# Loading w_out as four adjacent rows to a partition, with stage 1 taking w_in columns at a step of four

## The chip, the cores and the metric

One core of one Trainium2 chip. The time is the device time of one launch in microseconds; each kernel is run several times and the median is quoted with the range. Ratios are the mean time of one kernel's fast runs over the mean time of the other's fast runs of the same rounds, so they are not quite the ratios of the medians quoted beside them; the interval is 95%. A run more than 1.5% above the fastest of its kernel counts as slow and is left out of the ratios. TensorE is called PE in the views, its weight loads PEld, GpSimd POOL, SyncE SP; st, h, o and acc are the names of the tiles that matmuls write.

## The reference

Sliding-window attention (window 64) over q, k, v of 8 batches x 8 heads x 576 positions x 64, then a two-layer block on the 4608 x 512 result:

```python
def _moe_ref(x, w_in, w_out):            # x 4608 x 512, w_in 512 x 2048, w_out 2048 x 512
    h = x @ w_in
    relu6 = np.clip(h + 3.0, 0.0, 6.0)
    g = h * relu6 / 6.0
    return (g @ w_out).astype(np.float32)
```

The change concerns only the two weight matrices. The order of the 2048 hidden columns is free, as long as stage 1 (x @ w_in) and stage 2 (g @ w_out) use the same one.

## The kernel before

Both weights lie in SBUF as bf16, each in one tile, brought by four loads of 1 MB (fp32 in HBM, cast in the DMA) from GpSimd's queue. A w_in load brings a block of 512 columns for all four row groups g; the block's four pieces of a partition therefore lie 2048 elements apart.

```python
win16 = consts.tile([P, NG, FF], BF16, name="win16")       # P = 128, NG = 4, FF = 2048
wout16 = consts.tile([P, NFC, DM], BF16, name="wout16")    # NFC = 16, DM = 512

def load_w_in(f0, f1, g0, g1):
    return nc.gpsimd.dma_start(
        out=win16[:, g0:g1, f0:f1],
        in_=moe_w_in[g0 * P : g1 * P, f0:f1].rearrange("(g p) f -> p g f", p=P))

def load_w_out(c0, c1):
    return nc.gpsimd.dma_start(
        out=wout16[:, c0:c1, :],
        in_=moe_w_out[c0 * P : c1 * P, :].rearrange("(c p) j -> p c j", p=P))
# ... the order on GpSimd's queue (casts between them cut) ...
w_in = [load_w_in(0, 512, 0, NG)]
w_in.append(load_w_in(512, 1024, 0, NG))
w_in.append(load_w_in(1024, 1536, 0, NG))
ld = LoadsForPE(1, nc.gpsimd)
ld.main(0, 0, 4)          # q of the second batch, 512 KB
ld.main(1, 0, 4)          # k, 512 KB
w_in.append(load_w_in(1536, 2048, 0, NG))
ld.rest()
w_out = [load_w_out(0, 4)]
# ... stage 1, for a block T of 512 tokens and a group fc of 128 hidden columns ...
for g in gs:
    nc.tensor.matmul(
        hT, lhsT=win16[:, g, fc * P : (fc + 1) * P],
        rhs=xT[:, g, t0 : t0 + TB], start=(g == 0), stop=(g == NG - 1))
```

The program does not write its waits. A tracker in the framework puts semaphore waits where it sees an instruction touch a stretch of a tile that earlier instructions wrote. That is the author's reading: the compiled lists below show the waits, not how they are found. The order of instructions is fixed by the program.

The softmax here doesn't subtract the row's maximum and nothing guards it: scores larger than these inputs give would overflow.

Of the kernel before, what the change touches and what calls it, by code (L numbers as in the profile page):

```python
# [24 lines left out]
def kernel(  # L25
# [10 lines left out]
    P = nc.NUM_PARTITIONS  # L36
# [191 lines left out]
    win16 = consts.tile([P, NG, FF], BF16, name="win16")  # L228
    wout16 = consts.tile([P, NFC, DM], BF16, name="wout16")

    def load_w_in(f0, f1, g0, g1):
        return nc.gpsimd.dma_start(
            out=win16[:, g0:g1, f0:f1],
            in_=moe_w_in[g0 * P : g1 * P, f0:f1].rearrange("(g p) f -> p g f", p=P),
        )

    def load_w_out(c0, c1):
        return nc.gpsimd.dma_start(
            out=wout16[:, c0:c1, :],
            in_=moe_w_out[c0 * P : c1 * P, :].rearrange("(c p) j -> p c j", p=P),  # L240
        )


# [272 lines left out]
    def s1_bank(fc, T):  # L516
        if T == 0:
            if fc in (6, 7, 14, 15):
                return (ps_o, ps_acc)[fc % 2].tile([P, 512], F32, name=("o", "acc")[fc % 2])[:]
            if fc in (8, 9, 12, 13):  # L520
                return ps_st.tile([P, 2, 512], F32, name=f"st{fc % 2}")[:, 0, :]
            return h_bank()[:]
        if T == 1:
            return turn()
        if T == 2:
            if fc in (8, 9):
                return ps_st.tile([P, 2, 512], F32, name=f"st{fc % 2}")[:, 0, :]
            if fc in (6, 7, 12, 13):
                return (ps_o, ps_acc)[fc % 2].tile([P, 512], F32, name=("o", "acc")[fc % 2])[:]
            return h_bank()[:]  # L530
        if T > 1 and fc < 2:
            return ps_st.tile([P, 2, 512], F32, name=f"st{fc}")[:, 0, :]
        if fc % 4 > 1:
            return h_bank()[:]
        return (ps_o, ps_acc)[fc % 4].tile([P, 512], F32, name=("o", "acc")[fc % 4])[:]
# [3 lines left out]
    def turn(tr=False):  # L539
        i = turns[0] % 6  # L540
        turns[0] += 1
        shape, dt = ([P, 1024], BF16) if tr else ([P, 512], F32)
        if i < 2:
            return ps_h.tile(shape, dt, name=h_name())[:]
        if i < 4:
            return (ps_o, ps_acc)[i - 2].tile(shape, dt, name=("o", "acc")[i - 2])[:]
        return ps_st.tile([P, 2, shape[1]], dt, name=f"st{i - 4}")[:, 0, :]
# [12 lines left out]
    def s1(T, first=()):  # L560
        t0 = T * TB
        gT = gpool.tile([P, NFC, TB], BF16, name="gT")
        gTs[T] = gT

        def mms(fc, hT, gs):
            for g in gs:
                nc.tensor.matmul(  # L567
                    hT, lhsT=win16[:, g, fc * P : (fc + 1) * P],
                    rhs=xT[:, g, t0 : t0 + TB], start=(g == 0), stop=(g == NG - 1),
                )  # L570

        def gate(out, hT, shape):
            t1 = (t1pool, t2pool)[len(shape) - 2].tile(shape, BF16, name=f"t{len(shape) - 1}")
            nc.scalar.activation(out=t1[:], in_=hT, func=RELU, bias=half[:], scale=1.0 / 6.0)  # L574
            nc.vector.scalar_tensor_tensor(  # L575
                out=out, in0=t1[:], scalar=1.0, in1=hT, op0=MIN, op1=MULT,
            )

        if T == 1:
            hTs = [turn() for fc in range(4)]  # L580
            for gs in first:
                for fc in range(4):
                    mms(fc, hTs[fc], gs)
                yield
            for fc in range(4):
                mms(fc, hTs[fc], (NG - 1,))
                gate(gT[:, fc, :], hTs[fc], [P, TB])
                yield
        elif first:
            sts = [ps_st.tile([P, 2, 512], F32, name=f"st{u}") for u in range(2)]  # L590
            for gs in first:
                for fc in range(4):
                    mms(fc, sts[fc // 2][:, fc % 2, :], gs)
                yield
            for u in range(2):
                for fc in (2 * u, 2 * u + 1):
                    mms(fc, sts[u][:, fc % 2, :], (NG - 1,))
                gate(gT[:, 2 * u : 2 * u + 2, :], sts[u][:], [P, 2, TB])
                yield
                yield  # L600
        for fc in range(4 if first else 0, NFC):
            hT = s1_bank(fc, T)
            mms(fc, hT, range(NG))
            gate(gT[:, fc, :], hT, [P, TB])
            yield
# [17 lines left out]
    def s2(T, order):  # L623

        gT, accs = gTs[T], {}
        for ts, f0, f1 in order:
            if T == NTB - 1 and ts == 3:
                yield from last(gT, ts) if f0 == 0 else ()
                continue
            if f0 == 0:  # L630
                accs[ts] = h_bank()[:] if T == 0 and ts < 2 else next(oa)
            for fc in range(f0, f1):
                nc.tensor.matmul(  # L633
                    accs[ts], lhsT=gT[:, fc, ts * P : (ts + 1) * P], rhs=wout16[:, fc, :],
                    start=(fc == 0), stop=(fc == NFC - 1),
                )
            if f1 == NFC:
                osb = osbp.tile([P, DM], F32, name="osb")
                acopy(out=osb[:], in_=accs[ts])  # L639
                u0 = T * TB + ts * P  # L640
                if T:
                    nc.sync.dma_start(out=out[u0 : u0 + P, :], in_=osb[:])
                else:
                    held.append((u0, osb))
            yield
# [62 lines left out]
    for g in range(NG):  # L708
        cast_pairs(bt, st, 2 * g, 2)
    bt.cast_v(vst0, 0, 2, pcopy)  # L710
    w_in = [load_w_in(0, 512, 0, NG)]
    bt.cast_v(vst0, 2, 4, pcopy)
    bt.cast_v(vst0, 4, 6, pcopy)
    w_in.append(load_w_in(512, 1024, 0, NG))
    bt.cast_v(vst0, 6, 8, pcopy)
    w_in.append(load_w_in(1024, 1536, 0, NG))
    ld = LoadsForPE(1, nc.gpsimd)
    ld.main(0, 0, 4)
    ld.main(1, 0, 4)
# [3 lines that stand above are left out]
    pcopy(out=bt.V[0:SR, KB - 1, :, 0:D], in_=bt.V[SR:P, KB - 2, :, 0:D])  # L723

# [44 lines left out]
    m = s1(0, ((0, 1), (2,)))  # L769
# [19 lines left out]
    bt.cast_qk(st, 1, 0, 4, pcopy)  # L789
    bt.cast_rest(st, pcopy)  # L790
    w_out += [load_w_out(4 * i, 4 * i + 4) for i in (1, 2)]
    rst0, rvst0 = load_rest_of_first()
    cast_pairs(bt, st, 4, 4)
    w_out.append(load_w_out(12, 16))
    vst1, insv = load_v_by_head(1)
    run(m, 12)
# [26 lines left out]
    m = s2(0, BY_PART)  # L823
# [150 lines left out]
```

## Time and profile before

| | before |
|---|---|
| median (range), 3 runs | 309.83 us (309.78 to 311.08) |
| profiled span (of a run of 311.6 us) | 309.7 us |
| TensorE busy | 298.7 us, 96% |
| TensorE's wait for w_in | 0.5 us, once |
| TensorE's wait for w_out | 0.7 us, once |
| first stage-1 matmul on record | 18.26 us |
| first stage-2 matmul | 34.10 us |

The lines themselves are in the prediction below. In a line of waits the numbers are the total, the count and the longest; in a line of the chain, start, duration and what ran.

### The profile page before, as it was taken

The numbers are of one execution on the slowest core, as the hardware profiler recorded it, in microseconds if no ns is written. First come the engines' busy times: TensorE is split into PE (matmuls) and PEld (weight loads), VectorE is DVE, ScalarE is ACT, GpSimd is POOL, SyncE is SP. The second block draws the span as 40 slices with busy tenths as digits, with TensorE's granted clock in tenths as the row PEclk, the third lists the DMA queues.
The fourth block names the chain that finished last, engine by engine and source line by source line (L and its number), as shares of the span: only waits on it lengthen the run. The fifth ranks groups of instructions, "written<-read, shape, count | busy, mean of one in ns | idle before, by whom it ended". The sixth has DMA issues, their size and how long they took to land.

```text
span 309.7 us, 5637 instructions
## 1 busy us (share of the span) xinstructions
PE 298.7 (96%) x2158; PEld 150.4 (49%) x2194; DVE 176.2 (57%) x331; ACT 176.2 (57%) x266; POOL 98.7 (32%) x137
## 2 busy tenths in 40 slices
PE   8889999999999998999999999999999999999995
PEld 3454455544554463445444554455445544444444
DVE  4559645585737771677257834784377527306700
ACT  3848646686638851794179516961588157317711
POOL 5873865544434255017401740066000000000000
PEclk9999999999999999999999999999999999999999
DMA  7999997999999999999999999999910630010011
GB/s 245 205 218 251 247 220 164 250 217 263 201 195 251 221 200 204 209 219 205 194 246 206 206 185 237 215 196 204 225 37 0 134 89 0 34 70 34 0 70 68
DMA packets 140379, 52.94 MB, mean 171 GB/s; under 512 B 127584, under 2 KB 135136, under 8 KB 140352
## 3 DMA queue, kind: packets, MB, share of 16 engines
q1 hardware_dynamic: 134112, 42.94, 69.3%
q0 software_dynamic: 5824, 9.31, 14.3%
q8 instruction: 17, 0.28, 0.4%
q10 hardware_dynamic: 416, 0.33, 0.3%
q14 instruction: 10, 0.08, 0.1%
HBM read 36.83 MB, written 9.44 MB: 149 GB/s over the span
## 4 chain that ended last, share of the span: by engine, by line
PE 81%; DMA 9%; SPq 3%; POOL 2%; issue 2%; DVE 1%; ACT 1%; POOLq 0%
PE o L633 17%; PE h L567 17%; PE acc L633 15%; PE acc L567 6%; PE o L567 6%; PE st L567 6%; DMA wout<-in_moe_w_out_dram 5%; PE st L364 4%; PE h L633 2%; PE h L394 2%; DMA xT<-opg 2%; DMA qst<-in_q_dram 2%; PE h L399 1%; SPq L499 1%; DMA vst<-in_v_dram 1%
## 5 line engine op out<-in xcount | busy, mean ns | idle before, releaser
L567 PEld LDWEIGHTS <-win 128*128 128x128 bf16 x576 | 55.0, 98 | 65.9 <-issue 2.2
L633 PEld LDWEIGHTS <-gT 128*128 128x128 bf16 x560 | 51.4, 98 | 57.4 <-DMA wout<-in_moe_w_out_dram 1.2
L633 PE MATMUL o<-wout,gT 128*128 128x512 bf16 x261 | 64.3, 380 | 0.7 <-issue 0.3
L567 PE MATMUL h<-xT,win 128*128 128x512 bf16 x254 | 62.4, 379 | 0.3
L633 PE MATMUL acc<-wout,gT 128*128 128x512 bf16 x245 | 58.3, 379 | 0.9 <-issue 0.5
L372 ACT ACTIVATE pT<-st 128x768 bf16<-128x768 f32 x64 | 48.5, 808 | 17.3 <-PE st L364 17.2
L575 DVE SCALAR_TENSOR_TENSOR gT<-t,st 128x512 bf16<-128x512 bf16 (+1 forms) x26 | 19.5, 767 | 57.3 <-ACT t L574 57.2
L575 DVE SCALAR_TENSOR_TENSOR gT<-t,h 128x512 bf16<-128x512 bf16 x65 | 43.8, 685 | 11.6 <-ACT t L574 11.3
L574 ACT ACTIVATE t<-h,half 128x512 bf16<-128x512 f32 x65 | 43.9, 692 | 7.7 <-PE h L567 7.5
L382 DVE TENSOR_TENSOR pT<-pT,mask 128x1536 bf16<-128x1536 bf16 x28 | 30.1, 1074 | 22.7 <-ACT pT L372 22.6
L263 POOL CAST qn<-qst 128x512 bf16<-128x512 f32 x24 | 16.7, 736 | 61.0 <-DMA qst<-in_q_dram 42.6
L639 ACT COPY osb<-acc 128x512 f32<-128x512 f32 x16 | 9.4, 587 | 43.0 <-PE acc L633 43.0
L567 PE MATMUL st<-xT,win 128*128 128x512 bf16 x116 | 28.5, 379 | 1.6 <-DMA xT<-opg 1.0
L639 ACT COPY osb<-o 128x512 f32<-128x512 f32 x17 | 10.0, 589 | 29.4 <-PE o L633 28.3
L567 PE MATMUL acc<-xT,win 128*128 128x512 bf16 x98 | 25.7, 379 | 0.1
L567 PE MATMUL o<-xT,win 128*128 128x512 bf16 x95 | 25.1, 379 | 0.3 <-ACT xT L445 0.3
L416 DVE TENSOR_TENSOR opg<-h,rec 128x320 bf16<-128x320 f32 x48 | 23.6, 491 | 1.7
L574 ACT ACTIVATE t<-st,half 128x512 bf16<-128x512 f32 (+1 forms) x26 | 19.3, 754 | 6.5 <-PE st L567 6.0
L253 POOL CAST V<-vst 128x2048 bf16<-128x2048 f32 (+1 forms) x10 | 13.9, 1390 | 24.6 <-DMA vst<-in_v_dram 22.5
L394 PEld LDWEIGHTS <-pT 128*128 128x128 bf16 x256 | 17.4, 97 | 7.8 <-DVE opg L416 0.9
L574 ACT ACTIVATE t<-acc,half 128x512 bf16<-128x512 f32 x25 | 17.2, 688 | 4.3 <-PE acc L567 3.6
L575 DVE SCALAR_TENSOR_TENSOR gT<-t,acc 128x512 bf16<-128x512 bf16 x25 | 17.1, 685 | 2.8 <-ACT t L574 2.8
(123 smaller groups left out, 300.9 us busy)
## 6 DMA issues: line engine op xcount, KB each, us to landing
out_dram<-osb SPq DMA_DIRECT2D x31, 256.0 KB, 2.5
qst<-in_q_dram SPq DMA_DIRECT2D x28, 256.0 KB, 4.8
vst<-in_v_dram SPq DMA_DIRECT2D x24, 256.0 KB, 5.8
kst<-in_k_dram SPq DMA_DIRECT2D x23, 256.0 KB, 5.5
win<-in_moe_w_in_dram POOLq DMA_DIRECT2D x4, 512.0 KB, 8.1
wout<-in_moe_w_out_dram POOLq DMA_DIRECT2D x4, 512.0 KB, 9.6
vst<-in_v_dram SPq DMA_DIRECT2D x14, 128.0 KB, 3.2
qst<-in_q_dram POOLq DMA_DIRECT2D x2, 512.0 KB, 11.8
```

Source lines behind the costliest of these rows:

```text
L253: copy(out=self.V[:, 0 : KB - 1, h0:h1, 0:D], in_=vst[:, 0 : KB - 1, h0:h1, :])
L263: pcopy(out=n[:, g, 0 : KB - 1, :, :].rearrange("p k h d -> p k (h d)"), in_=s[:, 0 : KB - 1, 2 * g : 2 * g + 2, :].rearrange("p k h d -> ...
L364: nc.tensor.matmul(st[:, h, o0 : o0 + n], lhsT=bt.KT[h * D : (h + 1) * D, g, k0 : k0 + P], rhs=bt.QT[h * D : (h + 1) * D, g, q0 : q0 + n], ...
L372: nc.scalar.activation(out=pT[:, :, 2 * u : 2 * u + 2, 0:QW], in_=st[:, :, 0:w].rearrange("p h (k w) -> p h k w", k=2), func=EXP, scale=scale,
L382: nc.vector.tensor_tensor(out=pT[:, :, :, 0:QW], in0=pT[:, :, :, 0:QW], in1=mask[:].rearrange("p (h k) w -> p h k w", h=2), op=MULT,)
L394: nc.tensor.matmul(ob, lhsT=pT[:, h, qb, 0:P], rhs=V[:, qb, 2 * g + h, :], start=True, stop=(qb == 0),)
L416: nc.vector.tensor_tensor(out=opgs[bt.b, g][:, 0:nb, h, :], in0=ov[:, :, 0:D], in1=rec[:, 0:nb].unsqueeze(2).to_broadcast([P, nb, D]), op= ...
L567: nc.tensor.matmul(hT, lhsT=win16[:, g, fc * P : (fc + 1) * P], rhs=xT[:, g, t0 : t0 + TB], start=(g == 0), stop=(g == NG - 1),)
L574: nc.scalar.activation(out=t1[:], in_=hT, func=RELU, bias=half[:], scale=1.0 / 6.0)
L575: nc.vector.scalar_tensor_tensor(out=out, in0=t1[:], scalar=1.0, in1=hT, op0=MIN, op1=MULT,)
L633: nc.tensor.matmul(accs[ts], lhsT=gT[:, fc, ts * P : (ts + 1) * P], rhs=wout16[:, fc, :], start=(fc == 0), stop=(fc == NFC - 1),)
L639: acopy(out=osb[:], in_=accs[ts])
```

## The change

Intent: eight kilobytes of adjacent HBM for each partition in a w_out load, in place of four runs of 2 KB. Partition p of a load then holds rows 4p to 4p+3, so the hidden columns of stage 1 must come in that order too, which is a column step of four.

```diff
+    w_in_of = win16[:].rearrange("p g (u m c) -> p g u m c", m=P, c=4)
 ...
-            in_=moe_w_out[c0 * P : c1 * P, :].rearrange("(c p) j -> p c j", p=P),
+            in_=moe_w_out[c0 * P : c1 * P, :].rearrange("(p c) j -> p c j", p=P),
 ...
-                    hT, lhsT=win16[:, g, fc * P : (fc + 1) * P],
+                    hT, lhsT=w_in_of[:, g, fc // 4, :, fc % 4],
```

## The prediction

> **What bounds the kernel now.** I read the page's busy table, the chain of work that ended last, and the groups; then the waits of TensorE, the chain in order of time up to 60 us, TensorE's timelines, and the DMA packets in short stretches. First the page: the engine totals, the slices, the chain by engine.
>
> ```profile
> PE 298.7 (96%) x2158; PEld 150.4 (49%) x2194; DVE 176.2 (57%) x331; ACT 176.2 (57%) x266; POOL 98.7 (32%) x137
> ...
> PE   8889999999999998999999999999999999999995
> ...
> PE 81%; DMA 9%; SPq 3%; POOL 2%; issue 2%; DVE 1%; ACT 1%; POOLq 0%
> ```
>
> TensorE (PE) is busy in 298.7 of 309.7 us, evenly, and is four fifths of the chain. A change can win only from the 11 us in which it isn't, or lose by making its instructions follow each other more slowly. A busy PE need not be one at its peak, so I look at spacing. In the chain in order of time (start, duration, what; an entry ends where its successor takes over) stage 1 (L567) and stage 2 (L633) run like this:
>
> ```profile
> 187.29 1.73 PE st L567 x8
> 189.01 1.73 PE h L567 x8
> ...
> 208.04 2.59 PE acc L633 x12
> ```
>
> Eight stage-1 matmuls take 1.73 us, 216 ns each; twelve of stage 2 take 2.59 us, also 216 ns. So both stages already run at one matmul in 216 ns, with a weight load before each that costs nothing. How much room that load has shows in the groups (mean ns after the bar) and in the load timeline of a stretch of narrow matmuls:
>
> ```profile
> L567 PEld LDWEIGHTS <-win 128*128 128x128 bf16 x576 | 55.0, 98 | 65.9 <-issue 2.2
> ...
> 15.57 0.10 PEld L394 LDWEIGHTS <-pT 128*128 128x128 bf16 x1
> 15.60 0.10 PEld L399 LDWEIGHTS <-pT 128*128 128x128 bf16 x1
> 15.62 0.10 PEld L394 LDWEIGHTS <-pT 128*128 128x128 bf16 x1
> 15.65 0.10 PEld L399 LDWEIGHTS <-pT 128*128 128x128 bf16 x1
> ```
>
> A record of a load lasts 98 ns, but loads of the same 128x128 shape start every 25 to 30 ns here, each followed by a 65-column matmul. So 98 ns is a latency; a contiguous load occupies its path for 30 ns at most. In stage 1 it has 216 ns: a slack of about seven times.
>
> Where does w_out come in? The first 34 us of the chain end with its first load, and TensorE's waits show what that costs:
>
> ```profile
> 19.27 14.78 DMA wout<-in_moe_w_out_dram
> 34.10 1.04 PE h L633 x4
> ```
>
> ```profile
> PE h L633 <- DMA wout<-in_moe_w_out_dram: 0.7, 1, 0.7
> ```
>
> The chain charges 14.78 us to this DMA, about 5% of the span, but TensorE worked nearly throughout on stage 1 of the first block; it stood still for 0.7 us, once. That is all that an earlier w_out can give TensorE directly.
>
> [...]
>
> **The change part by part.** The instructions of each engine keep number, order and shape; only the address patterns of the four w_out loads and of 576 weight loads differ.
>
> *w_out loads.* Before, a load of 512 rows has 512 runs of 2 KB read, 1 KB written in bf16. After, 128 runs of 8 KB read, 4 KB written. How fast is the present form? From 26 to 27 us the software queue moved only weights:
>
> ```profile
> q0 software_dynamic: 200, 0.21, 121.9%
> ```
>
> 200 packets in 1 us on 16 engines is one packet in 80 ns per engine, 2048 bytes read in it: 25.6 GB/s per engine, 410 GB/s over 16. From 37 to 38 us, within w_out's second load, it is 196 packets, the same. [...] An estimate, then: a 1 MB load takes 512 x 80 / 16 = 2.56 us now[...]. The issue-to-landing times of 7.8 to 14.8 us are mostly the queue ahead of it.
>
> [...] The second (issued 31.46, landing after 7.8, so at 39.26 just as its first matmul starts) is behind the first in the queue[...]; third and fourth had about 1 us to spare[...]. [...] Issuing may get cheaper too: the four w_out issues take 772 ns each on GpSimd, while stores of 128 runs (L918) take 550; 4 x 0.22 = 0.9 us less on an engine that is 32% busy. Off the path: the queue was backlogged when the first was issued.
>
> *Stage 1 loads.* Let L be the time a strided load occupies its path. [...] If half or quarter rate, L is 60 to 120 ns: still under 216 ns, hidden behind 512-column matmuls. It shows only where stage 1 resumes after short work, because the load before the first matmul has little to hide behind. I counted changes into L567 in PE's timeline: 30, of which 7 follow a 512-column L633 and 23 follow narrow attention work. 23 x (30 to 90 ns) is 0.7 to 2.1 us at worst, less where the load is pulled ahead. I book 0 to 0.7 us, middle 0.2.
>
> Sum: 309.83 - 0.15 + 0.2, about 309.9 us. I choose 309.8, since the more likely case is that the load costs nothing.
>
> **Rivals.** (a) *The load becomes the bound.* [...] each of 576 pairs pays L - 216. Two per cent (6.2 us) needs L = 227 ns; 300 ns would add 48 us, 358 in all. Against it: the seven-fold slack[...]. For it: nothing in this trace has a strided load. (b) *A bigger win from DMA.* Four times fewer packets could shorten the queue enough to erase the whole 0.7 us wait and bring forward what stands behind it: the second batch's values, whose casts end only 0.1 to 0.5 us before their matmuls at 52.7 to 54.6 us. That would make about 308.8 to 309.1. Against it: [...] software-queue traffic is over by 70 us, with TensorE dense after that. (c) *The wait moves.* The longer packets lie in front of other transfers on the same engines, or spread worse over the 16 engines[...]. The hardware queue issued almost nothing from 15 to 48 us, so little stands there to be hurt; worth at most +0.3. (d) *Entry cost at its largest*, all 23 entries paying 90 ns: 311.9.
>
> **Range and chances.** Before itself ran from 309.78 to 311.08. Low end from (b) 308.8; high end from (d) with a little allowance below its worst, 311.6. Over 2% faster would need 6.2 us out of 11 us idle, only 0.7 of which hangs on w_out: 0.01. Over 2% slower needs (a): 0.06. Within 2%: 0.93.
>
> **What would show it.** Right: the software queue's packets fall by 3 x 512 = 1536 from 5824 to 4288; PE's wait for w_out is 0.5 to 0.6 us; stage-1 groups still take 1.73 us for eight; the loads of L567 still last about 98 ns. If the wait is gone, (b) holds and the packet arithmetic was wrong. If L567's load records are longer but eight matmuls still take 1.73 us, the slack hid it, and entries into L567 show small gaps. If eight take clearly over 1.73 us, (a) holds and the step that the load stays fast is wrong. A packet count of about 4800 would say that runs are cut at 4 KB read.

The forecast's sum came to 309.83 - 0.15 + 0.2, about 309.9 us. The -0.15 (what each w_out load was to gain), and the wait of 0.5 to 0.6 us expected from it, stand as guesses without a trace. Rival (a) is the case that a load takes longer than the 216 ns between matmuls. One figure is a little off: the software queue still moved 0.59 MB from 70 to 72 us, and nothing later.

## The result, and the profile after

The changed kernel takes 324.63 us (321.97 to 325.92, 4 runs) against 309.80 us of the kernel before: ratio 1.046, interval 1.040 to 1.052. It is slower by 14 to 15 us, well outside the range on record.

The page of the changed kernel, slices (40 of 8.1 us, a digit is tenths: TensorE's busy share, then its granted clock) and queue of the w_out loads (packets, MB, share of time):

```profile
PE   7813999899999999999999999999999999999995
...
PEclk9985899999999999999999999999999999999999
...
q0 software_dynamic: 4288, 9.31, 13.3%
```

Everything is at the start: TensorE's third slice is a 1 and its fourth a 3, and its clock is lowered in the third, fourth and fifth. From the sixth slice on the row looks as before. The packet count is 4288, as predicted. The longest wait of TensorE, and the chain in order of time:

```profile
PE st L569 <- DMA win<-in_moe_w_in_dram: 12.0, 1, 12.0
```

```profile
17.00 12.55 DMA win<-in_moe_w_in_dram
29.70 3.15 PE st L569 x7
33.27 2.70 PE st L569 x8
35.97 1.73 PE h L569 x8
```

(L569 is the stage-1 matmul, L567 of before; L635 is L633.) Two things are to be seen. TensorE waits 12.0 us for the w_in load that was issued at 17.00, which is the fourth one, though the first 512 hidden columns need only the first. Before, it waited 0.5 us. And after the wait seven matmuls take 3.15 us and the next eight 2.70, where the later eight take 1.73. The same stretches of 10 us in both kernels, before first (columns: stretch, its length, busy us and count of PE, PEld, DVE, ACT, POOL, then the granted clock, the DMA share and GB/s):

```profile
20.00:30.00 10.00, 9.95 (x55) 4.76 (x54) 7.07 (x10) 8.26 (x12) 4.29 (x6) 1.00 1.19 257
30.00:40.00 10.00, 9.26 (x72) 4.75 (x72) 7.13 (x11) 6.25 (x9) 8.23 (x11) 1.00 1.16 251
```

```profile
20.00:30.00 10.00, 0.30 (x1) 0.14 (x2) 0.00 (x0) 0.00 (x0) 3.98 (x5) 0.57 1.15 254
30.00:40.00 10.00, 10.00 (x39) 4.63 (x38) 3.28 (x4) 4.67 (x7) 8.69 (x12) 0.74 1.04 257
```

TensorE does 1 matmul where it did 55, and the granted clock averages 0.57 and 0.74. DMA throughput is the same in both, 254 to 257 against 251 to 257 GB/s: the transfers as a whole are not slower, one is waited for. Read microsecond by microsecond, the clock of the changed kernel is 1.00 up to 21 us and 0.50 from 22 to 35 us.

The loss adds up from the two timelines of TensorE (start, duration, line and operation, in brackets the idle time before it), before first:

```profile
18.26 1.67 PE L567 MATMUL st<-xT,win 128*128 128x512 bf16 x7 [0.49 <-DMA win<-in_moe_w_in_dram]
21.72 1.89 PE L567 MATMUL h<-xT,win 128*128 128x512 bf16 x8
```

```profile
35.81 1.89 PE L569 MATMUL h<-xT,win 128*128 128x512 bf16 x8
47.28 1.03 PE L635 MATMUL h<-wout,gT 128*128 128x512 bf16 x4
```

The first stage-1 matmul on record after the wait starts at 29.70 and not at 18.26: +11.44. (The very first, of row group 0, has no record in either trace, so both are the second.) From there to the first matmul into tile h it is 6.11 us (35.81 - 29.70) and not 3.46 (21.72 - 18.26): +2.65. From there to the first stage-2 matmul 11.47 us (47.28 - 35.81) and not 12.38 (34.10 - 21.72): -0.91, of which 0.69 is the w_out wait, which is gone. That is +13.2 at the start of stage 2; the remaining stretch is 276.3 us and not 275.6, +0.7. Together 13.9, the difference of the spans. The profiled run of before (311.6 us) was itself 1.8 us above the median, so a rest of 0.7 us is within the scatter.

The compiled instruction lists, read with their waits, say who ordered the wait. TensorE's instructions 317 to 320, before:

```
317 L567 Ldweights win_162 [waits DMASW0_49]
318 L567 Matmult st_418<-xT,win_162 128x512
319 L567 Ldweights win_162
320 L567 Matmult st_418<-xT,win_162 128x512 [waits Activation_49]
```

and after:

```
317 L569 Ldweights win_162 [waits DMASW0_49]
318 L569 Matmult st_418<-xT,win_162 128x512
319 L569 Ldweights win_162 [waits DMASW5_49,DMASW2_49,DMASW1_49]
320 L569 Matmult st_418<-xT,win_162 128x512 [waits Activation_49]
```

The second weight load, that of row group 1, now also waits for the three other w_in loads. It reads nothing of theirs. Before, each later block of 512 columns had its own wait, where stage 1 reached it. In the built program one instruction of TensorE was added that only waits, for two of the three; the page counts 5638 instructions where it counted 5637.

### The profile page after: what moved, and what is told of

The parts are those of the page before. It is cut to its first block, busy times and chain, and to the rows that moved or that the text cites. A ratio compares the mean times of both kernels' runs of the same rounds, so it can differ in the third digit from the quotient of the medians.

```text
span 323.6 us, 5638 instructions
## 1 busy us (share of the span) xinstructions
PE 300.8 (93%) x2158; PEld 159.7 (49%) x2194; DVE 178.7 (55%) x331; ACT 176.3 (54%) x266; POOL 99.0 (31%) x137
## 3 DMA queue, kind: packets, MB, share of 16 engines
q0 software_dynamic: 4288, 9.31, 13.3%
## 4 chain that ended last, share of the span: by engine, by line
PE 85%; DMA 6%; DVE 2%; issue 1%; SPq 1%; POOL 1%; ACT 1%; POOLq 0%
PE o L635 18%; PE h L569 17%; PE acc L635 16%; PE st L569 9%; PE acc L569 7%; PE o L569 6%; DMA win<-in_moe_w_in_dram 4%; PE st L366 4%; PE h L635 2%; PE h L396 2%; DVE pT L384 2%; DMA qst<-in_q_dram 1%; PE h L401 1%; DMA vst<-in_v_dram 1%; ACT pT L374 1%
## 5 line engine op out<-in xcount | busy, mean ns | idle before, releaser
L569 PEld LDWEIGHTS <-win 128*128 128x128 bf16 x576 | 64.3, 114 | 69.4 <-issue 15.2
L635 PEld LDWEIGHTS <-gT 128*128 128x128 bf16 x560 | 51.4, 98 | 56.2
L635 PE MATMUL o<-wout,gT 128*128 128x512 bf16 x261 | 64.3, 380 | 0.7 <-issue 0.3
L569 PE MATMUL h<-xT,win 128*128 128x512 bf16 x254 | 62.6, 380 | 0.3
L635 PE MATMUL acc<-wout,gT 128*128 128x512 bf16 x245 | 58.3, 379 | 0.9 <-issue 0.5
L577 DVE SCALAR_TENSOR_TENSOR gT<-t,h 128x512 bf16<-128x512 bf16 x65 | 43.7, 684 | 11.6 <-ACT t L576 11.4
L384 DVE TENSOR_TENSOR pT<-pT,mask 128x1536 bf16<-128x1536 bf16 x28 | 32.3, 1155 | 21.7 <-ACT pT L374 21.7
L569 PE MATMUL st<-xT,win 128*128 128x512 bf16 x116 | 30.6, 404 | 12.1 <-DMA win<-in_moe_w_in_dram 12.0
L265 POOL CAST qn<-qst 128x512 bf16<-128x512 f32 x24 | 15.9, 701 | 76.5 <-DMA qst<-in_q_dram 56.3
L569 PE MATMUL acc<-xT,win 128*128 128x512 bf16 x98 | 25.7, 379 | 0.1
L569 PE MATMUL o<-xT,win 128*128 128x512 bf16 x95 | 25.1, 379 | 0.3 <-ACT xT L447 0.3
```

What stands on the lines that cost most here:

```text
L265: pcopy(out=n[:, g, 0 : KB - 1, :, :].rearrange("p k h d -> p k (h d)"), in_=s[:, 0 : KB - 1, 2 * g : 2 * g + 2, :].rearrange("p k h d -> ...
L384: nc.vector.tensor_tensor(out=pT[:, :, :, 0:QW], in0=pT[:, :, :, 0:QW], in1=mask[:].rearrange("p (h k) w -> p h k w", h=2), op=MULT,)
L569: nc.tensor.matmul(hT, lhsT=w_in_of[:, g, fc // 4, :, fc % 4], rhs=xT[:, g, t0 : t0 + TB], start=(g == 0), stop=(g == NG - 1),)
L577: nc.vector.scalar_tensor_tensor(out=out, in0=t1[:], scalar=1.0, in1=hT, op0=MIN, op1=MULT,)
L635: nc.tensor.matmul(accs[ts], lhsT=gT[:, fc, ts * P : (ts + 1) * P], rhs=wout16[:, fc, :], start=(fc == 0), stop=(fc == NFC - 1),)
```

## The experiments

Theory 1: the strided read makes the tracker see an overlap with all four w_in loads; TensorE waits for the last of them, its clock is lowered meanwhile, and nothing else costs much. Theory 2: the strided weight loads are slow by themselves. Theory 3: the long w_out runs hold other transfers up. Five results are wrong: four where one half of the change stands alone, and that of the sweep.

### blockmajor: the whole change, without the overlap

```diff
-    win16 = consts.tile([P, NG, FF], BF16, name="win16")
+    win16 = consts.tile([P, FF // 512, NG, 512], BF16, name="win16")
-    w_in_of = win16[:].rearrange("p g (u m c) -> p g u m c", m=P, c=4)
+    w_in_of = win16[:].rearrange("p u g (m c) -> p u g m c", c=4)
-            out=win16[:, g0:g1, f0:f1],
+            out=win16[:, f0 // 512, g0:g1, :],
-                    hT, lhsT=w_in_of[:, g, fc // 4, :, fc % 4],
+                    hT, lhsT=w_in_of[:, fc // 4, g, :, fc % 4],
```

> The changed kernel with one thing altered: the w_in tile is laid out block-major (four blocks of 512 columns outermost in a partition, then the four row groups), so that each of the four w_in loads fills one contiguous stretch and no strided read spans another load's stretch. The loads, the step of four in stage 1 and the long w_out runs stay. In the compiled instruction list the second weight load of stage 1 no longer waits for the other three w_in loads. Theory 1 (the loss is the added wait for all four w_in loads and the cold clock after it): 309.0 to 310.0 us, TensorE's wait for w_in at most 0.6 us, granted clock 1.00. Theory 2 (the strided weight loads themselves cost the time): 320 us or more, since they are unchanged. Theory 3 (the long w_out runs hold up other transfers): 320 us or more. In every case the stage-1 load records should stay at about 113 ns.

310.00 us (309.23 to 311.25, 6 runs), ratio 0.9993 to the kernel before, interval 0.9956 to 1.003; correct. The whole loss is gone, with the same step of four and the same long runs. The wait and the load records of its profile:

```profile
PE st L569 <- DMA win<-in_moe_w_in_dram: 0.5, 1, 0.5
```

```profile
L569 PEld LDWEIGHTS <-win 128*128 128x128 bf16 x576 | 64.1, 114 | 57.4 <-issue 2.2 <-DMA win<-in_moe_w_in_dram 0.7
```

The wait is back at 0.5 us, and the load records still last 114 ns, so they are not what cost 14 us. Theories 2 and 3 fall as the cause. One part of the expectation missed: the clock was 0.999 or 1.0 in only five of six runs, and 0.993 in the profiled one. Its stretch from 18 to 22 us has a clock of 0.57, which is 3.4 us at half. This spell of half clock is taken up below.

### waits_alone: the kernel before, with the waits added by hand

```diff
-                nc.tensor.matmul(
+                mm = nc.tensor.matmul(
                     hT, lhsT=win16[:, g, fc * P : (fc + 1) * P],
                     rhs=xT[:, g, t0 : t0 + TB], start=(g == 0), stop=(g == NG - 1),
                 )
+                if (T, fc, g) == (0, 0, 1):
+                    for ld_ in w_in[1:]:
+                        after(mm, ld_, "wait for all four")
```

> The kernel before, contiguous columns and short w_out runs, but with the second weight load of stage 1 made to wait for all four w_in loads; in the compiled list it waits for the same three semaphores as in the changed kernel. The result is correct. Theory 1: 322.5 to 325.5 us, a wait of about 12 us for w_in, a granted clock of about 0.98 and the first 15 stage-1 matmuls after it slow. Theory 2 or 3: 309.5 to 311 us, as neither a stride nor a long run is there.

323.94 us (321.58 to 326.76, 4 runs, of which the longest is left out of the ratio), ratio 1.0419, interval 1.036 to 1.0478; correct. Contiguous columns, short runs, and the loss is there: the wait by itself makes it. TensorE's timeline:

```profile
19.68 0.39 PE L567 MATMUL st<-xT,win 128*128 128x512 bf16 x1 [1.22 <-DMA win<-in_moe_w_in_dram]
30.38 3.14 PE L567 MATMUL st<-xT,win 128*128 128x512 bf16 x7 [10.30 <-DMA win<-in_moe_w_in_dram]
```

One matmul (row group 0) runs after its own load; the next waits 10.3 us, and seven take 3.14 us without any stride.

### stride_alone: the strided read alone, result wrong

```diff
 (the changed kernel, with the w_out load put back)
-            in_=moe_w_out[...].rearrange("(p c) j -> p c j", p=P),
+            in_=moe_w_out[...].rearrange("(c p) j -> p c j", p=P),
```

> The kernel before with the stage-1 part alone (single row-group-major w_in tile, step of four, w_out loaded as before); the result is wrong on purpose. Theory 1: 323 to 326 us, with a wait of about 12 us for w_in and the 0.7 us wait for w_out hidden behind it. Theory 2: the same time, but without the time being one stretch at 18 to 30 us. Theory 3: about 310 us.

323.77 us (322.37 to 324.42, 4 runs), ratio 1.0433, interval 1.0385 to 1.0481, with TensorE waiting 10.7 us for w_in in two waits, 10.5 the longer. The stage-1 half carries the loss, without any long run.

### wout_alone: the w_out load alone, result wrong

```diff
 (the kernel before)
-            in_=moe_w_out[...].rearrange("(c p) j -> p c j", p=P),
+            in_=moe_w_out[...].rearrange("(p c) j -> p c j", p=P),
```

> The kernel before with the w_out part of the change alone; the result is wrong on purpose, as stage 1 still takes contiguous columns. Theory 1: 309.0 to 309.7 us, the 0.7 us wait for w_out gone or smaller, nothing else. Theory 2: the same. Theory 3 (long runs hold up other transfers): clearly over 310, up to 324 us.

310.29 us (308.49 to 312.21, 6 runs), ratio 1.0007, interval 0.9954 to 1.0059. Theory 3 is out. The median missed the expected 309.0 to 309.7: three runs at a clock of 1.00 took 308.5 to 309.1 and three at 0.993 or 0.994 took 311.5 to 312.2, so the spell of half clock hides what the part gives. How fast the loads run shows in the software queue's packets (count, MB written, share) from 38 to 39 us, while w_out loads are under way:

```profile
q0 software_dynamic: 53, 0.21, 103.5%
```

53 packets of 4 KB written a microsecond against 196 to 200 of 1 KB before: 0.21 MB against 0.20 to 0.21. A quarter of the packets, nearly the same rate. Other microseconds between 29 and 39, partly with other transfers in them, carry 0.19 to 0.23 MB in this run, so a gain of a few per cent is not resolved.

### fourth_first: which load is waited for

```diff
 (the changed kernel)
     w_in.append(load_w_in(1024, 1536, 0, NG))
+    w_in.append(load_w_in(1536, 2048, 0, NG))
     ld = LoadsForPE(1, nc.gpsimd)
     ld.main(0, 0, 4)
     ld.main(1, 0, 4)
-    w_in.append(load_w_in(1536, 2048, 0, NG))
```

> The changed kernel with the fourth w_in load issued right after the third, ahead of the two 512 KB loads of q and k for the second batch. If TensorE waits for the last w_in load to land, the wait ends some 3 us sooner (two 512 KB transfers at about 350 GB/s leave the queue ahead of it): the first stage-1 matmul after the wait at about 26.5 us and not 29.7, wait 8 to 10 us, 320 to 322.5 us in all. If it waits for something else (the first load, or stage 1's other input), the wait stays 12 us and the time 324.

319.78 us (318.48 to 321.58, 4 runs), ratio 1.0286, interval 1.0241 to 1.0331; correct.

```profile
PE st L569 <- DMA win<-in_moe_w_in_dram: 8.7, 2, 7.1
```

```profile
27.21 3.15 PE L569 MATMUL st<-xT,win 128*128 128x512 bf16 x7 [7.13 <-DMA win<-in_moe_w_in_dram]
```

The waits for w_in shrink from 12.0 to 8.7 us because one transfer was moved forward: it is the last w_in load that ends the long one. The start after the wait is 27.21, which is 2.5 us sooner, though a little later than the 26.5 expected. (The 350 GB/s there are an estimate: in the changed kernel's profile the software queue moved 0.36 and 0.37 MB in the two microseconds from 22 to 24.) The median is a little below its range: it fell by 4.9 us, of which the sooner start explains about half; the rest was not followed.

### after_warm: the clock's part of the loss

```diff
 (the changed kernel)
     m = s1(0, ((0, 1), (2,)))
+    warm = next(oa)
+    next(oa)
+    for _ in range(54):
+        nc.tensor.matmul(warm, lhsT=xT[:, 0, 0:P], rhs=xT[:, 0, 0:TB], start=True, stop=True)
     run(m, 1)
```

> The changed kernel with 54 idle matmuls of 512 columns put into TensorE's queue ahead of stage 1, to fill the 12 us wait (54 x 216 ns = 11.7 us). The wait itself stays. If the second part of the loss is the clock that is lowered during the idle time and makes the first 15 stage-1 matmuls slow (3.15 + 2.90 us where the kernel before takes 1.67 + 1.89), the clock stays at 1.00 and 2.3 to 2.9 us come back: 321.0 to 322.5 us. If those matmuls are slow because of their strided loads or for a lack of inputs, nothing comes back: 324 to 325 us.

321.54 us (321.06 to 322.15, 4 runs), ratio 1.0358, interval 1.0326 to 1.039; correct. The idle matmuls fill the time, and the wait ends about as late (30.19 against 29.70):

```profile
17.73 11.83 PE L775 MATMUL o<-xT 128*128 128x512 bf16 x54
29.40 0.38 PE L569 MATMUL st<-xT,win 128*128 128x512 bf16 x1
30.19 1.68 PE L569 MATMUL st<-xT,win 128*128 128x512 bf16 x7 [0.41 <-DMA win<-in_moe_w_in_dram]
```

The seven matmuls now take 1.68 us, with the same strided loads; from there to tile h it is 3.46 us (33.65 - 30.19), exactly as in the kernel before; and the clock is 0.999 or 1.0 in every run. From 324.63 to 321.54 is 3.1 us; by ratios, 1.046 - 1.0358 is one per cent or 3.2 us. Those medians are of different rounds; the trace's own figure for this part is 2.65. So about 11.4 us of the loss is the wait, and the slow start after it is the lowered clock.

### stride_sweep: the strided loads by themselves, result wrong

```diff
 (the kernel before)
+    STEP = {3: 2, 4: 4, 5: 8, 6: 16}          # block T: column step
+    def w_cols(T, g, fc):
+        s = STEP.get(T, 1)
+        return win16[:].rearrange("p g (u m c) -> p g u m c", m=P, c=s)[:, g, fc // s, :, fc % s]
-                    hT, lhsT=win16[:, g, fc * P : (fc + 1) * P],
+                    hT, lhsT=w_cols(T, g, fc),
```

> The kernel before with column steps of 2, 4, 8 and 16 in the stage 1 of blocks 3, 4, 5 and 6 (all w_in loads have long landed there); wrong result on purpose. It measures the disputed cost by itself. If strided loads are hidden behind 512-column matmuls, eight stage-1 matmuls take 1.73 us at every step and only the load records grow: 98 ns at step 1, about 113 at 4, more at 8 and 16. If a step [...](8 and 16) makes loads slow enough to bind, eight take over 1.8 us there. Time 309.5 to 311.5 us.

310.08 us, one run. The load records of stage 1 in blocks 3 to 6, that is at steps of 2, 4, 8 and 16 (minimum/median/maximum in ns, one line for each stretch of time):

```profile
L572 PEld LDWEIGHTS <-win x63: 96/98/101, 122.0 to 136.4; 128*128 128x128 bf16 x63
L572 PEld LDWEIGHTS <-win x63: 112/113/133, 153.9 to 168.4; 128*128 128x128 bf16 x63
L572 PEld LDWEIGHTS <-win x62: 141/144/168, 185.9 to 200.3; 128*128 128x128 bf16 x62
L572 PEld LDWEIGHTS <-win x61: 141/145/178, 218.0 to 232.2; 128*128 128x128 bf16 x61
```

and the first eight matmuls of each of these blocks, from the chain:

```profile
122.12 1.73 PE st L572 x8
...
154.08 1.73 PE st L572 x8
...
185.87 1.73 PE st L572 x8
...
217.75 1.73 PE st L572 x8
```

The loads do get longer than the 98 ns that this run shows at a step of one (block 8, 280 to 292 us): by nothing at step 2, 15 ns at 4, some 46 at 8 and 16. Eight matmuls take 1.73 us at every step. The steps show only where stage 1 resumes after attention work: the same four matmuls take 0.97, 0.99, 1.02 and 1.02 us there in the chain at steps of 2, 4, 8 and 16.

### w_before, w_blockmajor, w_wout, w_stride: the small parts, with the clock held up

The spell of half clock appeared in one of six runs of blockmajor, three of six of wout_alone and, across its rounds, some of the kernel before. It follows a stretch in which TensorE's work is thin, from 15 to 18 us (busy 2.02 of 3 us in blockmajor's profile, 2.25 in wout_alone's). So the same four idle matmuls were put there in four kernels, which ran in the same rounds:

```diff
+    def fill(n, u=0):
+        t = ps_st.tile([P, 2, 512], F32, name=f"st{u}")
+        for _ in range(n):
+            nc.tensor.matmul(t[:, 0, :], lhsT=ident[:], rhs=maskneg[:, 0:512], start=True, stop=True)
+    fill(1)
     N_(bt, 2, oa)
     X_(bt, 1)
+    fill(1)
     N_(bt, 3, oa)
 ...
+    fill(2, 1)
     m = s1(0, ((0, 1), (2,)))
```

> The kernel before with four idle 512-column matmuls put into TensorE's thin stretch between 15 and 18 us. Some runs of every kernel without the added wait show one 3.4 us spell at half clock there (clock 0.993 to 0.995), which makes differences under a microsecond unreadable. If the spell comes from TensorE's low activity in that stretch, all runs now have a clock of 0.998 or more and scatter less; time 308.5 to 310.5 us, against 308.8 to 312.2 of the kernel before. If it comes from elsewhere, spells of 0.993 to 0.995 stay in some runs.

> The block-major version (full change without the added wait) with the same four idle matmuls. Against the filled kernel before: the w_out part should give -0.2 to -0.7 us, the strided loads +0.3 to +0.6 us (23 entries into stage 1 with a load record 15 ns longer are 0.35 us); sum -0.4 to +0.4 us.

> The w_out part alone (wrong result on purpose) with the same four idle matmuls. Against the filled kernel before: -0.2 to -0.7 us if the earlier landing takes away TensorE's wait for w_out; 0 if that wait moves to something else.

> The strided loads alone, block-major tile, w_out loaded as before (wrong result on purpose), with the same four idle matmuls. Against the filled kernel before: +0.3 to +0.6 us if the longer loads show where stage 1 is entered; 0 if they are hidden there too.

| 5 rounds, 6 runs each | median (range), us | mean, us | clock | result |
|---|---|---|---|---|
| kernel before, same rounds, 10 fast runs of 11 | 311.41 (309.86 to 317.08, all 11) | 311.85 | 0.989 to 1.0 | correct |
| w_before | 311.41 (310.83 to 312.20) | 311.46 | 1.0 | correct |
| w_wout: long w_out runs only | 311.00 (310.30 to 312.33) | 311.10 | 0.998 to 0.999 | wrong |
| w_stride: block-major tile, step of four only | 311.10 (310.83 to 312.61) | 311.40 | 0.999 to 1.0 | wrong |
| w_blockmajor: both | 310.88 (309.56 to 311.11) | 310.52 | 0.998 to 1.0 | correct |

All 24 filled runs had a clock of 0.998 or more, while four of the 11 runs of the kernel before in the same rounds lay between 0.989 and 0.995. So the spell depends on the thin stretch, as expected. It is not the only source of scatter: 3.4 us at half clock cost 1.7 us at most, and one run of the kernel before took 313.12 us at a clock of 1.0. The filling hardly changes the median, though; the expected 308.5 to 310.5 us for w_before was missed, as the kernel before, too, was about 1 us slower in these rounds than in the earlier ones.

The parts: long w_out runs give 311.10 - 311.46 = -0.4 without the step and 310.52 - 311.40 = -0.9 with it. The step gives -0.1 and -0.6, where +0.3 to +0.6 was expected. The runs of one kernel scatter by 0.6 to 0.7 us, so a difference of two means of six has a standard error of about 0.4 us (0.7 x the root of 2/6). The step costs nothing that can be seen; the long runs may help by some half a microsecond, which is not shown. The profiles do not settle it: TensorE's wait for w_out is 0.5 us in w_before and in neither version with long runs, but it is also absent in w_stride and stride_sweep, which have short runs.

w_blockmajor is the fastest correct version tried: 0.9956 of the kernel before, interval 0.9909 to 1.0002. That is the same within 2%, and its interval includes 1.

## Why the prediction was wrong

**The step that failed.** "The instructions of each engine keep number, order and shape; only the address patterns of the four w_out loads and of 576 weight loads differ." Order and shape were kept, and the number but for one instruction that only waits. The semaphore waits were not kept, and the prediction says nothing of them. With the step of four the second weight load waited for three more loads, and TensorE stood still for 12.0 us with no work added. The step was booked at nothing, and the waits it overlooked were worth +11.4 us of standing still and some 2.7 us of lowered clock.

**No rival named it.** The rivals asked what a slower load, a faster DMA or a moved w_out wait would do. The transfer at issue, w_in, is not touched by the change, and it was nowhere in the sum. Rival (a) gave 6% to "slower", but by a load that bounds the matmuls, and eight matmuls took 1.73 us at every step.

**Why the tracker did it** is partly inferred. The three waits appear with the step of four in the row-group-major tile, and vanish with the same step in the block-major tile; that is shown. That the test of a strided read takes the hull of each load's four pieces (all from the first element to the last) fits the list: the read of row group 0 lies below the hulls of loads 2 to 4, which begin at column 512 of group 0, and waits for one load; that of group 1 lies inside all three hulls, and waits for them. The hull cannot be the test of every read: before, the contiguous read of row group 1 lay inside the same hulls and had no such wait. The tracker's code was not looked into.

**What held.** The load stayed hidden: 1.73 us for eight at every step; its record lengthened (98 to 114 ns in the changed kernel), which the prediction gave as the sign of a slack that hid it. The w_out loads had little to gain: 0.20 MB a microsecond became 0.21, with 0.19 to 0.23 around it. No trace of before showed that; the run showed it. Packets fell from 5824 to 4288, 1536 fewer, so a run of 8 KB read and 4 KB written counted as one. The median issue of a w_out load fell from 765 to 564 ns, as guessed from the 128-run stores. In the changed kernel the wait for w_out went, but as stage 2 came 13 us later, not by a faster load.

**What was mis-sized besides.** The cost where stage 1 resumes was booked at 0 to 0.7 us and is not visible (-0.1 and -0.6 with an error of 0.4). The gain from w_out, booked at -0.15, measured -0.4 and -0.9, each with a standard error of 0.4; whether it is the prediction's size or nearer to rival (b) stays open.

**Left open.** The +0.7 us after the first stage-2 matmul in the changed kernel: one new wait of 1.3 us for a copy by VectorE stands in its list of waits, and it was not followed. Nor was it tried why the thin stretch loses the clock in some runs only: from 14 to 18 us TensorE was busy 3.02 of 4 us in blockmajor's profile and 3.26 in wout_alone's, which both lost it, and 3.08 in that of before, which kept 1.00.

## What to carry to other kernels

Before a layout change is called neutral, compare the compiled instruction lists with their waits: here a read with a step of four was ordered after three loads of the same tile that it never reads, a wait of 12.0 us where 0.5 stood before. Where a tile is filled by several loads, lay it out so that each load, and everything read from it, occupies one unbroken stretch (with that blockmajor took 310.00 us, against 324.63), or give each load a tile of its own (that second way was not tried here). Here a wait of 12 us cost 11.4 us of standing still and 2.7 us of slow clock after it, so look at the granted clock in the stretch that follows a long wait.
